# The first tile of an attention and mixing kernel put in written order: another order for the next batch, conversions dealt by a table, and three pairs of weight parts prepared ahead

## The chip, the cores and the metric

The kernel runs on one core of a Trainium2 chip. The metric is the device time of one execution in microseconds (us); the median of three runs before the change is 1008.54 us (1007.43 to 1009.77). The engines are TensorE (PE, with its weight loads PEld), VectorE (DVE), ScalarE (ACT) and GpSimd (POOL); SyncE (SP) issues most transfers. Each engine works through its own list of instructions in order; an instruction whose input is late holds all that are behind it on its engine.

## The reference, cut to what matters

Eight batches of 576 tokens and 512 columns (8 heads of 64). Two attentions in a row, a real part of a two-dimensional Fourier transform, a normalisation and a two-layer network:

```
p_packed = sm_attn(p, k, v)               # 32 packed rows per head
x = sm_attn(q, p_packed, p_packed)        # (B, S, 512) over all heads
u = x + real(fft(fft(x, axis=1), axis=2))
un = (u - mean(u)) / sqrt(var(u) + 1e-6)
out = u + relu(un @ w_ch1) @ w_ch2        # 512 -> 2048 -> 512
```

The two weights come as 64-bit floats: each element is fetched as two 32-bit words, and the kernel puts one fp32 number together from them.

## The kernel before, in words

**The network's tiles.** The 8 x 576 rows are 36 blocks of 128 rows, worked in 9 tiles of four blocks (`ffn`). A tile has 16 chunks of the hidden 2048 columns. For chunk j, `up(j)` multiplies the four turned blocks by a 512 x 128 piece of the first weight (12 matmuls of 128x512, into the one PSUM bank `ph`), ACT and DVE make the rectified result's two parts `hh` and `hl` from it, and `down(j)` multiplies these by a 128 x 512 piece of the second weight into the four banks `acc0` to `acc3` (again 12 matmuls). Every product is made of three, from a high and a low part of each operand. `down(j - 1)` stands behind `up(j)` in the program. At a tile's end the four banks are scaled, added to `u` and sent out, and the next tile's rows are turned (on PE as `untp`, or by transfers as `back`) and split into `uh` and `ul`.

**The weight parts.** `wsplits` is a generator: each `next(splits)` makes one pair `wr_h`, `wr_l` for the next piece, first weight and second weight in turn: a cast on ACT (L105) and a subtraction on POOL (L108). Six buffers hold them, so three pairs at most. Before the first `up` two pairs are made; after each `up` and each `down` one more. The pair that is made behind a product is thus used two products later.

**The mixing of the next batch.** While tile t runs, `front(t + 1)` makes the rows of batch t + 1: a generator that is taken one piece further at each of the 32 steps of a tile (`step(2 * j)` behind `up(j)`, `step(2 * j + 1)` behind `down(j - 1)`). Which piece comes at which step is written in the strings of `ORDER`: each letter is a part (s scores, t turned scores, p packed values, d their parts, g their spectrum, q queries, e and m the softmax's two halves, a its weights, f r h the folds), the digit the group of heads, and y a step's end. The first string is the prologue's (batch 0), the second that of batch 1, the third that of all later batches. The capitals S, X, U do both groups of heads in one part.

**The weights' conversion.** Batch 0's tile also has to put the weights together, for 16 chunks and two weights, which later tiles find ready in `w1f` and `w2f`. One conversion is a transfer of 512 KB into a staging place (`fetch`), two instructions on ACT (`top` L175 and `lows` L180) and one on DVE (`bits` L184). Staging places are parts of `w1f` and `w2f` that are not yet filled, two slots of `ubuf`, and two buffers `wst`. Two chunks are converted in the prologue; in the first tile `load_weights` converts one chunk (two parts) at every second step, up to chunk 15; the transfer of a part is issued with its conversion, or by the prologue's letter W for the first two chunks.

**What sets the order.** In the prologue and in the tiles 1 to 8 the order on PE, DVE, ACT and POOL is the program's (`tc.manual_schedule`). In tile 0 it is that of a scheduler that goes by its own costs, but for some ACT instructions that are kept in program order. The order on SP is the scheduler's everywhere. At the end of the conversions four DVE instructions (L193 to L200) compare one converted part against another way of making it.

Of the kernel before, what the change touches and what calls it, by code (L numbers as in the profile page):

```python
# [81 lines left out]
def tile_kernel(ctx, tc, kpT, qT, v, w1, w2, tabH, tabL, tabR, tabB, tabT, sel, ident_d, out):  # L82
# [103 lines left out]
    def load_weights(j):  # L186
        for n in range(2):
            tc.keep_in_program_order(top(j, n))
            proof = n == 1 and j == NJ - 1
            if proof:  # L190
                low = fetched[j, n][:, :, 0]
                want = work.tile([P, DM], I32, tag="tmp", name="want", bufs=3)
                nc.vector.tensor_scalar(want, low, 29, None, ALU.logical_shift_right)  # L193
            tc.keep_in_program_order(lows(j, n))
            if proof:
                off = small.tile([P, 1], F32, tag="nb", name="off")
                nc.vector.tensor_tensor(want, want, low, ALU.bitwise_xor)
                nc.vector.tensor_reduce(off, want, AX.X, ALU.max)
                st = stat_of[0, "E", 0]
                nc.vector.scalar_tensor_tensor(st[:, 2:3], off, 1e6, st[:, 2:3], ALU.mult, ALU.add)  # L200
# [836 lines left out]
```

## Time and profile before

| what | value |
|---|---|
| runs, median (lowest to highest) | 1008.54 us (1007.43 to 1009.77) |
| profiled execution, its own time | 1009.32 us |
| its span, first to last instruction | 1007.5 us |
| mean granted TensorE clock | 0.996 |
| moved from and to HBM | 55.58 MB read, 16.25 MB written |

The span runs from the first to the last instruction; the execution's own time is 1.8 us longer. A row of the view by stretches of time holds, from the left, the stretch, its length, the busy time of PE, PEld, DVE, ACT and POOL with the number of instructions, the granted clock, the share of the DMA engines and GB/s. A row of the timeline holds start, busy time of the group, engine, line, operation, destination and sources, and in brackets how long the engine sat idle before and whose event ended that. The busy time of a matmul is longer than its turn on PE, since they overlap: two 128x512 matmuls in a row start 0.23 us apart, though each has 0.39 us. So what a wait costs is read from the distance of two starts.

### The profile page before, as it was taken

The page shows a single profiled execution, that of the slowest core. Times are in us where ns is not written, and L with a number is a line of the kernel's source. Part 1 is how long each engine was busy: PE and PEld are TensorE (multiplying, and loading weights), DVE is VectorE, ACT ScalarE, POOL GpSimd, SP SyncE. Part 2 cuts the span into 40 slices and gives each one's busy share as a digit, 9 for nine tenths or more (in the row PEclk, how much of TensorE's full clock was granted, in tenths as well). Part 3 has the DMA queues.
Part 4 walks back from the last instruction along what each step waited for, and adds up shares of the span by engine and source line. Part 5 has one row for each costly group of instructions (what it writes and reads, how often), then busy time and mean ns, then how long its engine had stood idle before and what let it go on. Part 6 is the DMA issues. An engine that isn't in the chain of part 4 may idle for free.

```text
span 1007.5 us, 15129 instructions
## 1 busy us (share of the span) xinstructions
PE 972.9 (97%) x5706; PEld 792.4 (79%) x5706; DVE 592.7 (59%) x1187; ACT 441.4 (44%) x914; POOL 463.2 (46%) x413
## 2 busy tenths in 40 slices
PE   7899899999999999999999999999999999999998
PEld 4777577878877887788878888778778888887886
DVE  5865976578555946685657755694658452323112
ACT  4578465444444345343434443443433443233322
POOL 3236635454345534553545435543454354544443
PEclk9999999999999999999999999999999999999999
DMA  9337430410122003300231114110211010111001
GB/s 352 119 112 226 146 126 28 136 50 22 43 100 92 22 8 129 98 24 19 85 108 42 43 42 142 50 63 18 99 47 36 28 64 1 45 39 43 0 1 43
DMA packets 36938, 72.83 MB, mean 72 GB/s; under 512 B 4224, under 2 KB 18432, under 8 KB 36864
## 3 DMA queue, kind: packets, MB, share of 16 engines
q1 hardware_dynamic: 35856, 70.34, 20.6%
q0 software_dynamic: 1008, 1.51, 0.5%
q8 instruction: 45, 0.74, 0.3%
q14 instruction: 29, 0.24, 0.1%
HBM read 55.58 MB, written 16.25 MB: 71 GB/s over the span
## 4 chain that ended last, share of the span: by engine, by line
PE 74%; DVE 11%; issue 7%; POOL 4%; ACT 3%; DMA 1%; ACTq 0%; SPq 0%; POOLq 0%; DVEq 0%
PE ph L806 33%; PE acc L823 28%; POOL wr_l L108 3%; DVE turned L470 1%; PE po L367 1%; DVE turned L464 1%; PE s L306 1%; PE px L266 1%; PE px L264 1%; PE px L265 1%; DVE hl L813 1%; PE py L266 1%; PE e1tp L344 1%; PE pz L266 1%; PE pz L265 1%
## 5 line engine op out<-in xcount | busy, mean ns | idle before, releaser
L108 POOL TENSOR_TENSOR wr_l<-w1f,wr_h 128x512 fp32r<-128x512 f32 x144 | 188.7, 1313 | 395.4 <-ACT wr_h L105 391.5
L813 DVE SCALAR_TENSOR_TENSOR hl<-ph,hh 128x512 fp32r<-128x512 f32 x144 | 98.7, 685 | 303.6 <-ACT hh L812 303.3
L806 PE MATMUL ph<-uh,wr_h 128*128 128x512 f32 (+1 forms) x580 | 229.7, 396 | 9.8 <-DVE f L515 3.1
L108 POOL TENSOR_TENSOR wr_l<-w2f,wr_h 128x512 fp32r<-128x512 f32 x144 | 194.2, 1349 | 96.5 <-ACT wr_h L105 88.4
L823 PE MATMUL acc<-wr_l,hh 128*128 128x512 f32 x576 | 226.1, 393 | 6.5 <-POOL wr_l L108 6.4
L812 ACT ACTIVATE hh<-ph 128x512 fp32r<-128x512 f32 x144 | 86.1, 598 | 323.5 <-PE ph L806 323.5
L823 PE MATMUL acc<-wr_h,hh 128*128 128x512 f32 x576 | 226.3, 393 | 1.2 <-ACT wr_h L105 1.2
L806 PE MATMUL ph<-uh,wr_l 128*128 128x512 f32 (+1 forms) x580 | 226.6, 391 | 0.5 <-POOL wr_l L108 0.5
L806 PE MATMUL ph<-ul,wr_h 128*128 128x512 f32 (+1 forms) x580 | 226.3, 390 | 0.0
L823 PE MATMUL acc<-wr_h,hl 128*128 128x512 f32 x576 | 225.0, 391 | 0.0
L806 PEld LDWEIGHTS ph<-uh,wr_h 128*128 128x128 f32 x580 | 109.3, 188 | 46.3 <-issue 16.6
L823 PEld LDWEIGHTS acc<-wr_l,hh 128*128 128x128 f32 x576 | 108.2, 188 | 31.5 <-POOL wr_l L108 10.7
L806 PEld LDWEIGHTS ph<-uh,wr_l 128*128 128x128 f32 x580 | 109.3, 188 | 25.1 <-POOL wr_l L108 1.1
L823 PEld LDWEIGHTS acc<-wr_h,hh 128*128 128x128 f32 x576 | 108.1, 188 | 24.4 <-ACT wr_h L105 1.7
L823 PEld LDWEIGHTS acc<-wr_h,hl 128*128 128x128 f32 x576 | 108.1, 188 | 22.6
L806 PEld LDWEIGHTS ph<-ul,wr_h 128*128 128x128 f32 x580 | 109.3, 189 | 20.7
L105 ACT CAST wr_h<-w2f 128x512 fp32r<-128x512 f32 x144 | 89.3, 620 | 0.0
L105 ACT CAST wr_h<-w1f 128x512 fp32r<-128x512 f32 x144 | 88.4, 614 | 0.8 <-DVE w1f L184 0.6
L240 ACT ACTIVATE junk<-ubuf,stat 128x512 f32<-128x512 f32 x36 | 25.8, 719 | 53.3 <-DVE stat L235 53.3
L108 POOL TENSOR_TENSOR gl<-turned,gh 128x516 fp32r<-128x516 f32 x14 | 21.7, 1553 | 16.3 <-ACT gh L105 16.3
L682 DVE SCALAR_TENSOR_TENSOR ubuf<-qe,pe 128x512 f32<-128x512 f32 x32 | 27.1, 883 | 0.5
L470 DVE TENSOR_TENSOR turned<-turned 128x258 f32<-128x258 f32 x32 | 26.9, 881 | 0.4
(213 smaller groups left out, 1282.9 us busy)
## 6 DMA issues: line engine op xcount, KB each, us to landing
kp<-kpT SPq DMA_DIRECT2D x16, 608.0 KB, 4.9
out<-ubuf SPq DMA_DIRECT2D x36, 256.0 KB, 2.1
vt<-v SPq DMA_DIRECT2D x14, 640.0 KB, 4.8
wst<-w SPq DMA_DIRECT2D x17, 512.0 KB, 4.3
qt<-qT SPq DMA_DIRECT2D x14, 576.0 KB, 4.6
far<-unt SPq DMA_DIRECT2D x26, 256.0 KB, 2.0
back<-far SPq DMA_DIRECT2D x104, 64.0 KB, 2.0
ubuf<-w SPq DMA_DIRECT2D x9, 512.0 KB, 4.3
```

Source lines behind the costliest of these rows:

```text
L105: copied = nc.scalar.copy(hi, src)
L108: (lo_eng or nc.vector).tensor_tensor(lo, src, hi.bitcast(F32), ALU.subtract)
L240: nc.scalar.activation(junk, u, AF.Square, bias=st[:, 1:2], scale=-sign, accum_out=st[:, 2:3])
L264: nc.tensor.matmul(o, lh, rh, start=first, stop=False)
L265: nc.tensor.matmul(o, lh, rl, start=False, stop=False)
L266: nc.tensor.matmul(o, ll, rh, start=False, stop=last)
L470: TW[TA[min(b, 2)]].tensor_tensor(prod[0][:, t, :], prod[0][:, t, :], prod[1][:, t, :], ops[t])
L682: nc.vector.scalar_tensor_tensor(u_of[key], qe, sign, pe, ALU.mult, ALU.add, accum_out=stat_of[key][:, 0:1])
L806: nc.tensor.matmul(ph[:, t], l[:, c * P:(c + 1) * P], r[:, c, t], start=(k == 0), stop=(k == 11))
L812: nc.scalar.activation(hh[:, :T], ph[:, :T], AF.Relu)
L813: nc.vector.scalar_tensor_tensor(hl[:, :T], ph[:, :T], 0.0, hh[:, :T].bitcast(F32), ALU.max, ALU.subtract)
L823: nc.tensor.matmul(acc[i], l[:, w], r, start=(j == 0 and k == 0), stop=(j == NJ - 1 and k == 2))
```

## The change

Six things are changed.

1. **Order of tile 0.** Tile 0 is put in `tc.manual_schedule` like the others: PE, DVE, ACT and POOL follow the program.
2. **The next batch's pieces.** The second string of `ORDER` is dropped, and batch 1 uses the third one, that of the later batches, with S, X and U for both groups together.
3. **Conversions by a table.** `TAKES` says for each of tile 0's 32 steps how many of the 27 conversions that are left behind the prologue are made there: 16 of them at the steps 2 to 11, one each at 12, 13, 14, 16, 18 and 21 to 24.
4. **Staging by a table.** `STAGES` gives each of the 32 parts its staging place; nine are fetched by the prologue (letters W0 to W8 in place of W0 to W3), and `fetch_free`, called with each conversion, fetches ahead as soon as the place of the next part is free.
5. **Three pairs.** Before the first `up` three pairs of weight parts are made and not two, so that a pair made behind a product is used three products later, in every tile.
6. **Small ones.** In the prologue two `lows` and three `bits` stand earlier and the conversion of the part (2, 0) is added; the first `up` does its 12 matmuls in another order; the comparison (L193 to L200) is gone.

```diff
 ORDER = ("... v0 z0 T2 W4 W5 W6 W7 W8 q0 e0 p1 "
-         "... i64 j1 F1 u1 u2 u3 h1 J1 X0 "
-         "H1 P1",
-         "s0 s1 y y t0 y t1 y p0 y y y d0 p1 y q0 d1 y y g0 y g1 y e0 q1 e1 y m0 y m1 y a0 a1 y f0 r0 h0 y "
-         "y f1 r1 h1",
+         "... i64 j1 u1 u2 F1 u3 h1 J1 v1 v2 X0 "
+         "H1 v3 P1",
          "S y X y p0 p1 y d0 d1 y g0 y U y g1 y e0 y e1 y y m0 y a0 y m1 y a1 y f0 y r0 y h0 y f1 y r1 y "
          "h1 y y")
-STG0 = [-2, -2, -4, -4, -6, -6]
-STG1 = [9, None, None]
+STAGES = [-2, -2, -4, -4, -6, -6, 9, 0, 1, -2, -2, -4, -4, -6, -6, 9, 0, 1, ...]
+TAKES = [1, 1, 2, 1, 2, 2, 2, 1, 2, 1, 1, 2, 1, 1, 1, 0, 1, 0, 1, 0, 0, 1, 1, 1, 1, 0, ...]
...
+    def fetch_free():
+        while line:
+            j, n = line[0]
+            i = STAGES[2 * j + n]
+            if last_in.get((i, i < 0 and n)) in fetched:
+                break
+            fetch(j, n)
...
-    def load_weights(j):
-        for n in range(2):
-            tc.keep_in_program_order(top(j, n))
...
+    def load_weights(count):
+        for j, n in todo[:count]:
+            top(j, n)
+            lows(j, n)
             bits(j, n)
+            fetch_free()
+        del todo[:count]
...
-        for x in ORDER[min(b, 2)].split():
+        for x in ORDER[min(b, 1)].split():
...
-                    c, (l, r) = k // 3, ((wh, uh), (wh, ul), (wl, uh))[k % 3]
+                    if step < T:
+                        c, (l, r) = k % 4, ((wh, uh), (wl, uh), (wh, ul))[k // 4]
+                    else:
+                        c, (l, r) = k // 3, ((wh, uh), (wh, ul), (wl, uh))[k % 3]
...
             if at == "means":
+                top(LEAD, 0)
+                lows(LEAD, 0)
                 turn_blocks(0, 1)
...
-        bits(1, 0)
         turn_blocks(2, 3)
         cur.parts(2)
         cur.parts(3)
+        bits(*todo.pop(0))
         next(splits)
-        bits(0, 1)
-        bits(1, 1)
+        next(splits)
...
-            if t == 0 and i % 2 == 0 and i // 2 + LEAD < NJ:
-                load_weights(i // 2 + LEAD)
+            if t == 0:
+                load_weights(TAKES[i])
...
-        with tc.manual_schedule(engines=MANUAL) if t > 0 else nullcontext():
+        with tc.manual_schedule(engines=MANUAL):
             ffn(first, cur, step, nxt, t + 1 >= B)
```

Three places show the order that results. The first is PE where the prologue passes into tile 0: `untp` turns the four blocks, `pz` is the rest of batch 0's mixing (step 0), `ph` is the first `up`. Before:

```order
L763 MATMUL untp<-ident,un 128x128 x4
L264 MATMUL pz<-yh,tbh_94 128x258
L265 MATMUL pz<-yl,tbh_94 128x258
L763 MATMUL untp<-ident,un 128x128 x4
L266 MATMUL pz<-yh,tbl_96 128x258
L264 MATMUL pz<-yh,tbh_94 128x258
```

and with the change:

```order
L763 MATMUL untp<-ident,un 128x128 x8
L809 MATMUL ph<-uh,wr_h 128x256 x4
L809 MATMUL ph<-uh,wr_l 128x256 x4
L763 MATMUL untp<-ident,un 128x128 x8
L809 MATMUL ph<-ul,wr_h 128x256 x4
L809 MATMUL ph<-uh,wr_h 128x256 x4
L809 MATMUL ph<-uh,wr_l 128x256 x4
L809 MATMUL ph<-ul,wr_h 128x256 x4
L264 MATMUL pz<-yh,tbh_94 128x258
```

The 14 `pz` matmuls stood between the turned blocks and now stand behind the whole first `up`, whose products without `ul` come first.

The second place is DVE in the middle of tile 0, where batch 1's softmax is finished for the first group of heads (`s_1099`; its `d` and `z` products are on POOL), ahead of the folds. With the change:

```order
L194 SCALAR_TENSOR_TENSOR w1f<-w1f,ubuf 128x512
L816 SCALAR_TENSOR_TENSOR hl<-ph,hh 128x512
L243 TENSOR_SCALAR stat<-stat 128x1
L441 TENSOR_REDUCE z_1264<-s_1099 128x18
L442 TENSOR_SCALAR d_1265<-z_1264 128x18
L443 TENSOR_SCALAR z_1264<-z_1264 128x18
L444 RECIPROCAL z_1264<-z_1264 128x18
L194 SCALAR_TENSOR_TENSOR w2f<-w2f,wst 128x512
L484 STREAM_TRANSPOSE a<-s_1099 128x576
L194 SCALAR_TENSOR_TENSOR w1f<-w1f,wst 128x512
L816 SCALAR_TENSOR_TENSOR hl<-ph,hh 128x512
```

Before, the last group's transpose and the first group's folds stood together with two conversions in front of one `hl`:

```order
L482 TENSOR_TENSOR s_1265<-s_1265,z_1328 128x576
L184 SCALAR_TENSOR_TENSOR w1f<-w1f,wst 128x512
L184 SCALAR_TENSOR_TENSOR w2f<-w2f,ubuf 128x512
L484 STREAM_TRANSPOSE a<-s_1265 128x576
L528 MEMSET f 128x3x2
L547 SCALAR_TENSOR_TENSOR xl<-eo,xh 128x256
L549 TENSOR_TENSOR ol<-eo,oh 128x256
L515 TENSOR_TENSOR f<-eo 128x2x3x15
L519 TENSOR_TENSOR f<-a 128x3 x2
L515 TENSOR_TENSOR f<-eo 128x2x3x15
L526 COPY f<-eo 128x2x3
L813 SCALAR_TENSOR_TENSOR hl<-ph,hh 128x512
```

The conversions have moved ahead of the folds, and the transpose `a` stands between two `hl` behind a chain on POOL.

The third place is ACT at the end of a later tile (tile 1), from the last `hh` on; `back` and `untp` are the next tile's rows. Before:

```order
L812 ACTIVATE hh<-ph 128x512
L105 CAST uh<-back 128x4x128 x2
L105 CAST wr_h<-w2f 128x512
L105 CAST wr_h<-w1f 128x512
L105 CAST uh<-back 128x4x128
L105 CAST uh<-untp 128x4x128
L105 CAST wr_h<-w1f 128x512
```

and with the change:

```order
L815 ACTIVATE hh<-ph 128x512
L103 CAST uh<-back 128x4x128 x2
L103 CAST wr_h<-w1f 128x512 x2
L103 CAST uh<-back 128x4x128
L103 CAST uh<-untp 128x4x128
L103 CAST wr_h<-w2f 128x512
```

The cast of the last piece of the second weight, `wr_h<-w2f`, stood behind two casts of `uh` and is no longer there: it is made one product earlier, ahead of `hh`.

More of the change, by code (lines that the diff above doesn't have):

```diff
@@ L1 @@
-from contextlib import ExitStack, nullcontext
+from contextlib import ExitStack
 import numpy as np
@@ L38 @@
 TL = (0, 0, 0)
-ORDER = ("K0 K1 V0 I0 Q0 V1 W0 Q1 B0 W1 W2 W3 i70 s0 x0 s1 i40 t0 x1 p0 b0 T0 t1 n0 w0 u0 d0 T1 i20 v0 z0 T2 q0 e0 p1 "
-         "b1 i80 l0 d1 w1 w2 w3 m0 q1 a0 e1 g0 i122 f0 r0 F0 l1 m1 n1 g1 i203 a1 j0 h0 J0 H0 P0 f1 r1 i64 j1 F1 u1 u2 u3 h1 J1 X0 "
-         "H1 P1",
-         "s0 s1 y y t0 y t1 y p0 y y y d0 p1 y q0 d1 y y g0 y g1 y e0 q1 e1 y m0 y m1 y a0 a1 y f0 r0 h0 y "
-         "y f1 r1 h1",
+ORDER = ("K0 K1 V0 I0 Q0 V1 W0 Q1 B0 W1 W2 W3 i70 s0 x0 s1 i40 t0 x1 p0 b0 T0 t1 n0 w0 u0 d0 T1 i20 v0 z0 T2 W4 W5 W6 W7 W8 q0 e0 p1 "
+         "b1 i80 l0 d1 w1 w2 w3 m0 q1 a0 e1 g0 i122 f0 r0 F0 l1 m1 n1 g1 i203 a1 j0 h0 J0 H0 P0 f1 r1 i64 j1 u1 u2 F1 u3 h1 J1 v1 v2 X0 "
+         "H1 v3 P1",
          "S y X y p0 p1 y d0 d1 y g0 y U y g1 y e0 y e1 y y m0 y a0 y m1 y a1 y f0 y r0 y h0 y f1 y r1 y "
          "h1 y y")
-STG0 = [-2, -2, -4, -4, -6, -6]
-STG1 = [9, None, None]
+STAGES = [-2, -2, -4, -4, -6, -6, 9, 0, 1, -2, -2, -4, -4, -6, -6, 9, 0, 1, -2, -2, -4, -4, 9, 0, 1, -2, -2, 9, 0, 1, 9, 0]
+TAKES = [1, 1, 2, 1, 2, 2, 2, 1, 2, 1, 1, 2, 1, 1, 1, 0, 1, 0, 1, 0, 0, 1, 1, 1, 1, 0, 0, 0, 0, 0, 0, 0]
 LEAD = 2
@@ L124, in tile_kernel @@
     idles = [psf.tile([P, 512], F32, tag="ph", name="idle")]
-    stages = (STG0 + STG1 * 40)[:2 * NJ]
     tbh = [cpool.tile([P, KT], F32R, name=f"tbh{t}") for t in range(2)]
@@ L153, in spot @@
         return t[:, 0:size].rearrange("p (a n) -> p a n", a=shape[1])
+    line = [(j, n) for j in range(NJ) for n in range(2)]
+    last_in = {}
     def fetch(j, n):
-        i = stages.pop(0)
-        if i is None:
+        assert line.pop(0) == (j, n)
+        i = STAGES[2 * j + n]
+        assert last_in.get((i, i < 0 and n)) not in fetched
+        last_in[i, i < 0 and n] = j, n
+        if i < 0:
+            st = spot(n, i, [P, 512, 2]).bitcast(I32)
+        elif i < 2:
             st = work.tile([P, 512, 2], I32, tag="wst", name="wst", bufs=2)
-        elif i < 0:
-            st = spot(n, i, [P, 512, 2]).bitcast(I32)
         else:
@@ L164, in fetch @@
         fetched[j, n] = st
+    def fetch_free():
+        while line:
+            j, n = line[0]
+            i = STAGES[2 * j + n]
+            if last_in.get((i, i < 0 and n)) in fetched:
+                break
+            fetch(j, n)
     def chunk(j, n):
@@ L169, in top @@
     def top(j, n):
-        if (j, n) not in fetched:
-            fetch(j, n)
         high, c = fetched[j, n][:, :, 1], chunk(j, n)
@@ L184, in bits @@
         nc.vector.scalar_tensor_tensor(c, c, 3, low, ALU.logical_shift_left, ALU.bitwise_or)
-    def load_weights(j):
-        for n in range(2):
-            tc.keep_in_program_order(top(j, n))
[L189 to L200, printed above, removed]
+    todo = [(j, n) for j in range(LEAD, NJ) for n in range(2)]
+    def load_weights(count):
+        for j, n in todo[:count]:
+            top(j, n)
+            lows(j, n)
             bits(j, n)
+            fetch_free()
+        del todo[:count]
     u_of, stat_of, place_of, free = {}, {}, {}, list(range(NU))
```

## The prediction

> **What bounds the kernel now.** I read the first page, the stretches by tile, PE's waits, and then the timelines around the waits. Page and stretches (one row for tile 0 from its first whole `up`, one each for tiles 1 and 2):
>
> ```profile
> span 1007.5 us, 15129 instructions
> PE 972.9 (97%) x5706; PEld 792.4 (79%) x5706; DVE 592.7 (59%) x1187; ACT 441.4 (44%) x914; POOL 463.2 (46%) x413
> 53.00:176.26 123.26, 114.02 (x658) 88.70 (x656) 87.23 (x170) 80.62 (x165) 61.93 (x54) 0.99 0.41 130
> 176.26:283.81 107.55, 106.81 (x650) 87.81 (x648) 72.28 (x147) 47.18 (x100) 49.51 (x42) 1.00 0.18 59
> 283.81:391.36 107.55, 106.80 (x649) 87.76 (x648) 70.87 (x143) 46.48 (x98) 50.30 (x43) 1.00 0.17 60
> ```
>
> PE sets the end: it is busy 97% and its tiles follow each other without a break. So only what shortens PE's own list or its waits counts. Tile 0 takes 123.3 us where tile 1 takes 107.55 with the same kind of work: nearly 16 us more. The other engines are busier in tile 0 (DVE 87 against 72, ACT 81 against 47) but not full over the whole of it. PE's waits in tile 0, and then from tile 1 to the end (total, times, longest):
>
> ```profile
> PE ph L806 <- ACT wr_h L105: 2.9, 1, 2.9
> PE acc L823 <- POOL wr_l L108: 1.7, 3, 0.9
> PE ph L806 <- DVE hl L813: 1.5, 1, 1.5
> PE py L264 <- ACT fh L538: 1.5, 1, 1.5
> PE acc L823 <- ACT wr_h L105: 1.2, 1, 1.2
> ...
> PE acc L823 <- POOL wr_l L108: 4.8, 7, 0.8
> PE ph L806 <- DVE f L515: 3.1, 2, 1.6
> ```
>
> Tile 0 has 8.8 us of them, most between 107 and 133 us, where DVE's list carries the folds and conversions at once. Later, one kind comes back seven times: the last `down` of tiles 1 to 7 waits for POOL's `wr_l`.
>
> **Tile 0, by the length of tile 1.** With the change tile 0 has the calls of tile 1 in the order of tile 1, so the PE list of tile 1 is the measure of it, from the first `pz` behind the first `up` to the next tile's first `ph`:
>
> ```profile
> 176.26 0.40 PE L806 MATMUL ph<-uh,wr_h 128*128 128x512 f32 x1
> 178.99 0.28 PE L264 MATMUL pz<-yh,tbh 128*128 128x258 f32 x1
> 283.81 0.39 PE L806 MATMUL ph<-uh,wr_h 128*128 128x512 f32 x1
> ...
> 279.32 0.48 PE L823 MATMUL acc<-wr_h,hh 128*128 128x512 f32 x1
> 279.67 0.48 PE L823 MATMUL acc<-wr_l,hh 128*128 128x512 f32 x1
> ```
>
> From 178.99 to 283.81 are 104.8 us. Tile 0 turns all four of its successor's blocks on PE, tile 1 only one: 12 transposes more. Between the last two rows stands one transpose, and they are 0.35 us apart where 0.23 is usual: 0.12 each, 1.4 us together. Tile 1 holds 0.6 us of a wait at its end that goes (below). So tile 0 without new waits lasts 104.8 + 1.4 - 0.6 = 105.6 us from its first `pz`.
>
> That `pz` now stands behind the first `up`. Two rows say when this can end:
>
> ```profile
> 48.26 1.33 ACT L888 ACTIVATE un<-ubuf,stat 128x512 f32<-128x512 f32 x2 [1.61 <-DVE stat L235]
> 53.44 0.59 ACT L105 CAST uh<-untp 128x512 fp32r<-128x512 f32 x1 [0.23 <-PE untp L763]
> 57.76 0.73 PE L823 MATMUL acc<-wr_h,hh 128*128 128x512 f32 x2 [1.19 <-ACT wr_h L105]
> ```
>
> The added `top` and `lows` of part (2, 0) need 1.1 us of ACT (start to start 0.56 each, below) and stand where ACT idled 1.61 us: nothing, with DVE's statistics as the cover; without it 1.1 us, on the path. The earlier `lows` and `bits` fall into the time in which ACT and DVE wait for the fold's high part; nothing too. The last `uh` is ready at 53.44 + 0.59 = 54.0; the second half of `up`, 12 half-wide matmuls at 0.12, ends at 55.5. The 1.19 us before 57.76 go, since the third pair's cast now stands ahead of `hh`. So tile 1 would begin at 55.5 + 105.6 = 161.1 and not at 176.26: **15.1 us less**, without new waits. This holds the shorter scores of both groups together and the lost half clock behind the longest wait:
>
> ```profile
> 116.10 0.55 PE L806 MATMUL ph<-uh,wr_h 128*128 128x512 f32 x1 [2.88 <-ACT wr_h L105]
> 119.82 0.40 PE L806 MATMUL ph<-uh,wr_h 128*128 128x512 f32 x1
> ```
>
> Nine starts in 3.72 us where 0.23 each is usual: 1.7 us lost after PE had idled 2.88.
>
> **The tile ends.** Here is one of the seven, on PE, ACT and POOL:
>
> ```profile
> 495.08 0.39 PE L823 MATMUL acc<-wr_h,hh 128*128 128x512 f32 x1
> 496.28 0.50 PE L823 MATMUL acc<-wr_l,hh 128*128 128x512 f32 x1 [0.81 <-POOL wr_l L108]
> 492.56 0.60 ACT L812 ACTIVATE hh<-ph 128x512 fp32r<-128x512 f32 x1 [1.18 <-PE ph L806]
> 493.05 1.13 ACT L105 CAST uh<-back 128x512 fp32r<-128x512 f32 x2
> 494.08 0.62 ACT L105 CAST wr_h<-w2f 128x512 fp32r<-128x512 f32 x1
> 494.78 1.44 POOL L108 TENSOR_TENSOR wr_l<-w2f,wr_h 128x512 fp32r<-128x512 f32 x1 [3.93 <-ACT wr_h L105]
> ```
>
> The cast stands behind `hh` and two `uh`, so POOL ends at 496.2 and PE's second matmul starts 1.20 us after its first, 0.97 late. With three pairs this cast and its `wr_l` are made a whole product (12 matmuls, 2.74 us) earlier: 2.74 of room against 0.97 of lateness. The 4.8 us of waits cost some 0.16 more each by that same pair of starts (0.97 against 0.81): 4.8 + 7 x 0.16 = **5.9 us less**. What is late next is nothing by these rows; the new pair's buffer comes free only at the product's end, so its cast now waits for PE, with the next step's ACT work behind it: 47 us of ACT in 107 leave room for that.
>
> **What written order may cost in tile 0.** Sixteen conversions stand in the steps 2 to 11, five chunks. Their prices, and the rows of the POOL chain:
>
> ```profile
> 113.27 0.66 ACT L175 ACTIVATE w1f<-wst 128x512 f32<-128x512 f32 x1
> 114.38 0.66 ACT L175 ACTIVATE w2f<-ubuf 128x512 f32<-128x512 f32 x1
> L184 DVE SCALAR_TENSOR_TENSOR w1f<-w1f 128x512 int32<-128x512 int32 x2 | 1.4, 682 | 0.0
> L184 DVE SCALAR_TENSOR_TENSOR w1f<-w1f,wst 128x512 int32<-128x512 int32 x8 | 7.1, 887 | 5.6 <-ACT wst L180 5.5
> L184 DVE SCALAR_TENSOR_TENSOR w2f<-w2f 128x512 int32<-128x512 int32 x3 | 3.1, 1053 | 0.0
> L445 POOL TENSOR_TENSOR s<-s,d 128x576 f32<-128x576 f32 x1 | 1.3, 1337 | 0.0
> L108 POOL TENSOR_TENSOR wr_l<-w1f,wr_h 128x512 fp32r<-128x512 f32 x17 | 22.6, 1330 | 34.0 <-ACT wr_h L105 30.9 <-DVE d L442 3.1
> L482 POOL TENSOR_TENSOR s<-s,z 128x576 f32<-128x576 f32 x1 | 1.2, 1162 | 0.8 <-DVE s L422 0.8
> L484 DVE STREAM_TRANSPOSE a<-s 128x576 f32<-128x576 f32 x2 | 1.5, 772 | 0.0
> ...
> wst<-w SPq DMA_DIRECT2D x17, 512.0 KB, 4.3
> ```
>
> Five chunks last 5 x 107.55 / 16 = 33.6 us. ACT does tile 1's work in them, 47.18 x 5 / 16 = 14.7, and 16 x 1.11 of conversions (113.27 to 114.38): 32.5 of 33.6. DVE: 72.28 x 5 / 16 = 22.6 and 16 x 0.68 to 0.89: 33.5 to 36.8. So DVE runs level or up to 3.2 us over; I take the middle, 1.6. Behind it comes the chain of the first group: DVE's `z` and `d` (about 1.0), then on POOL `s<-s,d` 1.34, a `wr_l` 1.33, `s<-s,z` 1.16, then on DVE `a` 0.77, a conversion 0.68 and only then `hl` 0.69, all in one line because DVE waits in front of `a`: 7.0 us between two `hl`. PE needs the next one after an `up` and a `down`, 2 x 2.74 = 5.5: 1.5 us late. For the folds behind it I add 1.4, the size of one of today's waits there. New waits: 1.6 + 1.5 + 1.4 = **4.5 us**, spread, so no lost clock. Bounds: nothing, if the slack of `ph` takes them; 12 us, if each of 27 conversions takes 1.05 on DVE and not 0.68 (10.0) and the chain's 1.5 comes on top, rounded up. I take a value at the lower part, since the waits today came with two conversions and the folds in one chunk, which is what is pulled apart. Transfers: nine parts stand ready from the prologue, each takes 4.3 us to land, and its place is free several steps before its turn: nothing. The dropped comparison stands in DVE idle time: nothing.
>
> [...]
>
> **The sum.** 15.1 + 5.9 - 4.5 = 16.5 us less. Of the profiled execution's 1009.32 that leaves 992.8; it stood 0.8 above the median, so 992 to 993: I say **993 us**.
>
> **The rivals.**
> 1. *The two waits of 1.6 us spread.* They stand in tiles 5 and 6 where `hl` comes late behind DVE instructions that take longer while a `wr_l` runs, as here the second against the first:
>
> ```profile
> 666.34 0.48 DVE L733 TENSOR_SCALAR unp<-ubuf,stat 128x512 f32<-128x512 f32 x1
> 672.51 1.57 DVE L733 TENSOR_SCALAR unp<-ubuf,stat 128x512 f32<-128x512 f32 x1
> ```
>
> Three pairs move every `wr_l`; if one such wait falls in each of tiles 1 to 7, 5 x 1.7 = 8.5 us come back: 1001.5. For it: the same list gave a wait in two tiles and none in five, so the phase decides. Against: the number of `wr_l` is the same.
> 2. *Tile 0 is bound by DVE.* New waits of 12 us, the bound above: 1000.5. For it: DVE is level with PE in five chunks. Against: over the whole tile it is not full.
> 3. *The third pair isn't really held*, because its cast waits for a buffer and is then as late as before: the tile ends keep their 5.9 us: 999. Against: it has a whole product more.
> 4. *Slower.* One mechanism: in tile 0's written order ACT's and DVE's conversions stand in front of `hh` and `hl`, and what they take shows on PE instead of beside it. A conversion is 1.11 + 0.68 = 1.8 us; it decides from the point where more than 21.0 / 27 = 0.78 us of each is seen. At half, 24 us: 1012. For it: both engines' lists are nearly full there. Against: the two work on different conversions at once, and `ph` leaves them one `down` of room each chunk.
>
> **How the numbers follow.** The forecast has 0.56, by itself 988 (no new waits) to 998; the rivals in their order 0.14, 0.14, 0.06 and 0.10. A measurement of this kernel tells about 0.2% from no change, 2 us. The forecast and rivals 1 to 3 are faster, together 0.90, less 0.04 for a tail of rival 2 that ends near the old time; slower is rival 4. Range: 987 to 1003 leaves out rival 4 and the edges of the others.
>
> **What would show it.** Tile 1's first `ph` near 166 us and not 176 (161 without new waits); no wait of `acc` on POOL's `wr_l` at the tile ends, tiles of some 106.8 us and not 107.55; in tile 0 short waits of `ph` on `hl` around chunks 6 to 8; no slow clock there. Tiles 1 to 7 of over 108 us would show rival 1; a wait of `acc` that stays, rival 3; tile 0 longer than 123 us, rival 4, and the forecast wrong.

## The result, and the profile of the changed kernel

| | kernel before | changed kernel |
|---|---|---|
| runs, median (lowest to highest) | 1008.98 us (1007.43 to 1009.98) | **999.36 us** (996.71 to 1002.41) |
| ratio, 95% interval | | **0.9908** (0.9884 to 0.9932) |
| profiled execution: its own time, span | 1009.32, 1007.5 us | 1002.41, 1000.6 us |
| tile 1's first `ph` starts at | 176.26 us | 178.95 us |
| from there to the end of the span | 831.2 us | 821.7 us |

The kernel before was run five times in all here; the three runs of the first table are among them. The time fell by 9.6 us, and 993 us were forecast, with 987 to 1003 as the range. The last two rows say more than the first: the whole gain stands behind tile 0. Tile 0 and the prologue, from which 10.6 us were expected, take 2.7 us longer in the profiled execution, which is the slowest of the five.

From the changed kernel's page, and two of its stretches (tile 0 from its first `pz` to tile 1's first `ph`, then tile 1 to tile 2's first `ph`; the columns are as before):

```profile
PE 970.3 (97%) x5706; PEld 797.6 (80%) x5706; DVE 565.3 (56%) x1183; ACT 450.9 (45%) x914; POOL 472.3 (47%) x413
58.75:178.95 120.20, 109.84 (x651) 88.74 (x649) 78.07 (x161) 78.88 (x159) 62.55 (x54) 0.97 0.35 115
178.95:285.32 106.37, 106.37 (x650) 87.78 (x648) 67.88 (x146) 47.84 (x100) 52.00 (x44) 1.00 0.18 61
```

Tile 1 has no idle PE left (106.37 busy of 106.37) and is 1.2 us shorter than the 107.55 of the kernel before. Tile 0 has 10.4 us of idle PE and a mean clock of 0.97. PE's waits, first three kinds from the list of the whole changed kernel, then (last two rows) all that is left from tile 1 on:

```profile
PE ph L809 <- DVE hl L816: 7.6, 5, 2.2
PE ph L809 <- DVE stat L243: 3.2, 1, 3.2
PE s2Tt L306 <- DMA qt<-qT: 1.9, 1, 1.9
...
PE ph L809 <- DVE hl L816: 3.0, 2, 1.5
PE ph L809 <- DVE ul L106: 0.5, 1, 0.5
```

The seven waits of `acc` on `wr_l` are gone. So is a kind that the prediction did not count, six waits of `ph` on the transposed scores, in the kernel before from tile 1 on:

```profile
PE ph L806 <- DVE s L422: 2.3, 6, 0.4
```

The reason is in the groups by line for the same stretch, the kernel before first (two rows), then the changed one:

```profile
L470 DVE TENSOR_TENSOR turned<-turned 128x258 f32<-128x258 f32 x24 | 21.7, 944 | 0.4
L429 DVE TENSOR_TENSOR s<-s,m 128x576 f32<-128x576 f32 x12 | 11.1, 924 | 0.4
L429 DVE TENSOR_TENSOR s<-s,m 128x576 f32<-128x576 f32 x12 | 15.9, 1328 | 0.4
L470 DVE TENSOR_TENSOR turned<-turned 128x258 f32<-128x258 f32 x24 | 9.2, 424 | 0.4
```

The join `turned` (L470) stands on DVE right ahead of the transposes that free the bank for which `ph` waits. It took 944 ns on the mean where a `wr_l` ran on POOL beside the first of each two (414 ns at the shortest, 1483 at the longest), and takes 424 now, with no `wr_l` beside it. The `wr_l`, made one product earlier, runs beside L429 instead, which takes longer there (924 to 1328 on the mean) and which nothing on PE waits for. So the same overlap of DVE and POOL is there as before, and here its move worked for the change. With 6 x 0.16 us for these waits (an estimate by the tile end in the prediction, where a wait of 0.81 us made the next start 0.97 late), their 2.3 us and the 5.9 us of the tile ends make 9.2 of the 9.6 us.

**What tile 0 lost.** The largest wait there ends at 108.92. On ACT, DVE and PE, with the stretch by which ACT is judged:

```profile
95.00:110.00 15.00, 11.83 (x53) 9.48 (x52) 9.88 (x16) 13.54 (x27) 9.57 (x8) 1.00 0.39 115
100.31 0.69 ACT L432 ACTIVATE s<-s 128x576 f32<-128x576 f32 x1 [1.40 <-POOL s L429]
105.25 0.64 ACT L185 ACTIVATE w2f<-w2f 128x512 f32<-128x512 f32 x1
106.89 0.65 ACT L190 ACTIVATE ubuf<-ubuf 128x512 int32<-128x512 uint8 x1
107.44 0.57 ACT L815 ACTIVATE hh<-ph 128x512 fp32r<-128x512 f32 x1
108.18 0.68 DVE L816 SCALAR_TENSOR_TENSOR hl<-ph,hh 128x512 fp32r<-128x512 f32 x1
108.92 0.50 PE L809 MATMUL ph<-uh,wr_h 128*128 128x512 f32 x1 [3.17 <-DVE stat L243]
```

The row names `stat`, a small instruction behind `hl`; what is late is `hl`, because `hh` stands on ACT behind two conversions (the row at 105.25 begins them, that at 106.89 ends them). ACT comes to them late: it is busy 13.5 of these 15 us, and of the 1.46 us in which it is not, 1.40 stand in one piece ahead of 100.31, where it waits for a subtraction of the scores on POOL. So two things make this wait, ACT's conversions and the scores' way over POOL; the experiments below take them apart. The next wait, 2.25 us at 116.90, is the chain that the prediction had written down:

```profile
109.62 0.37 DVE L442 TENSOR_SCALAR d<-z 128x18 f32<-128x18 f32 x1
110.43 1.63 POOL L445 TENSOR_TENSOR s<-s,d 128x576 f32<-128x576 f32 x1
112.02 1.30 POOL L106 TENSOR_TENSOR wr_l<-w1f,wr_h 128x512 fp32r<-128x512 f32 x1
113.28 1.15 POOL L482 TENSOR_TENSOR s<-s,z 128x576 f32<-128x576 f32 x1
114.47 0.78 DVE L484 STREAM_TRANSPOSE a<-s 128x576 f32<-128x576 f32 x1 [3.43 <-POOL s L482]
116.17 0.68 DVE L816 SCALAR_TENSOR_TENSOR hl<-ph,hh 128x512 fp32r<-128x512 f32 x1
```

From `hl` to `hl` are 116.17 - 108.18 = 8.0 us, where 7.0 were forecast. The other new stops of PE in tile 0 are 2.1 us at 83 (by the row of waits the second transfer of queries; e4 below corrects that), 1.6 us at 129 and 1.0 us at 136 (folds in front of `hl`), by the starts of its matmuls. With 3.3 and 2.4 us for the two above that makes 10.4 us, not 4.5. On top of it come stretches at half clock: over 5 us the granted clock is 0.76 and 0.78 from 40 and from 50 us, 0.70 from 85 and 0.77 from 115, where the kernel before has one such stretch (0.66 from 115).

### The profile page after: what moved, and what is told of

It reads as the page before. It is cut to its first block, busy times and chain, and to the rows that moved or that the text cites. A ratio compares the mean times of both kernels' runs of the same rounds, so it can differ in the third digit from the quotient of the medians.

```text
span 1000.6 us, 15241 instructions
## 1 busy us (share of the span) xinstructions
PE 970.3 (97%) x5706; PEld 797.6 (80%) x5706; DVE 565.3 (56%) x1183; ACT 450.9 (45%) x914; POOL 472.3 (47%) x413
## 3 DMA queue, kind: packets, MB, share of 16 engines
q1 hardware_dynamic: 35856, 70.34, 20.5%
## 4 chain that ended last, share of the span: by engine, by line
PE 86%; DVE 9%; ACT 2%; DMA 1%; issue 1%; POOL 1%; SPq 0%; ACTq 0%; POOLq 0%; DVEq 0%
PE ph L809 37%; PE acc L826 35%; DMA w1f<-w 1%; PE po L367 1%; DVE hl L816 1%; PE px L266 1%; PE px L264 1%; DVE s L482 1%; PE px L265 1%; PE py L266 1%; PE py L265 1%; PE py L264 1%; PE pz L264 1%; PE pz L265 1%; PE pz L266 1%
## 5 line engine op out<-in xcount | busy, mean ns | idle before, releaser
L106 POOL TENSOR_TENSOR wr_l<-w2f,wr_h 128x512 fp32r<-128x512 f32 x144 | 188.5, 1309 | 307.8 <-ACT wr_h L103 303.8
L106 POOL TENSOR_TENSOR wr_l<-w1f,wr_h 128x512 fp32r<-128x512 f32 x144 | 200.7, 1394 | 185.3 <-ACT wr_h L103 170.0
L872 DVE SCALAR_TENSOR_TENSOR ubuf<-acc,stat,ubuf 128x512 f32<-128x512 f32 x36 | 24.5, 742 | 2.2 <-PE acc L826 2.2
L106 DVE TENSOR_TENSOR yl<-py,yh 128x258 fp32r<-128x258 f32 x32 | 13.3, 426 | 19.1 <-ACT yh L103 18.2
L244 POOL TENSOR_TENSOR stat<-stat,mhalf 128x1 f32<-128x1 f32 x36 | 22.9, 649 | 0.8 <-DVE stat L243 0.8
```

Source lines behind the costliest of these rows:

```text
L106: (lo_eng or nc.vector).tensor_tensor(lo, src, hi.bitcast(F32), ALU.subtract)
L244: nc.gpsimd.tensor_tensor(st[:, 2:3], st[:, 2:3], mhalf, ALU.pow)
L872: nc.vector.scalar_tensor_tensor(u, acc[i], stat_of[key][:, 2:3], u, ALU.mult, ALU.add)
```

## The experiments

Theory A, formed on this comparison: the later tiles' 9.6 us are the pairs' alone; tile 0's order was worth about 15 us on PE's list and gave them back through waits (a chain over POOL, ACT's list of conversions) and the half clock behind some of them (6.8 us from 30 us on, 1.7 in the kernel before). The rivals are in the expectations. All twelve runs:

| run | median, us | ratio to the kernel before (95%) | tile 1's first `ph` |
|---|---|---|---|
| changed kernel | 999.36 | 0.9908 (0.9884 to 0.9932) | 178.95 |
| e1_pairs_only | 999.14 | 0.9901 (0.9886 to 0.9916) | 175.33 |
| e2_two_pairs | 1009.42 | 1.0006 (0.9991 to 1.0021) | 176.38 |
| e3_chain_on_dve | 996.81 | 0.9876 (0.9858 to 0.9895) | 175.14 |
| e4_queries_first | 1000.20 | 0.9911 (0.9884 to 0.9937) | 178.03 |
| e5_one_each | 997.76 | 0.9886 (0.9870 to 0.9903) | 173.45 |
| e6_later_tiles_engines | 995.09 | 0.9856 (0.9839 to 0.9872) | 170.55 |
| e7_prologue_back | 997.98 | 0.9888 (0.9872 to 0.9905) | 176.9 |
| e8_prologue_pz | 995.39 | 0.9859 (0.9845 to 0.9874) | 170.8 |
| e9_folds_kept_free | 991.30 | 0.9818 (0.9803 to 0.9833) | 167.43 |
| e10_more_early | 992.49 | 0.9830 (0.9817 to 0.9844) | 169.4 |
| e11_free_at_transposes | **988.98** | **0.9797** (0.9784 to 0.9811) | 164.48 |
| e12_old_pieces | 1005.98 | 0.9964 (0.9950 to 0.9978) | 182.54 |

### The pairs without the order, and the order without the pairs

e1, an edit of the kernel before:

```
             if t == 0 and i % 2 == 0 and i // 2 + LEAD < NJ:
                 load_weights(i // 2 + LEAD)
+            if t == 0 and i == 29:
+                next(splits)
```

> The kernel before, with one edit: in chunk 14 of tile 0 one more pair of weight parts is made ready, so that tiles 1 to 7 hold three pairs; tile 0's order and the prologue stay. Theory A (the later tiles' gain is the pairs' alone, tile 0 gained nothing): no wait of acc on wr_l at the tile ends, from tile 1's first ph to the end 821.7 us instead of 831.2, tile 1's first ph still near 176, the whole at 0.990 to 0.991 of the kernel before, level with the changed kernel. Theory B (the pairs give only the waits seen of acc, 4.8 us, or the predicted 5.9, and the rest of the later tiles' 9.6 comes with the written order): 825 to 826 us and 0.994 to 0.995. If a third pair is not really held: 831 us and 1.000.

e2, an edit of the changed kernel, at the end of the prologue:

```
         next(splits)
-        next(splits)
```

> The changed kernel with two pairs held instead of three, everything else as changed. Theory A: the waits of acc on wr_l come back at the tile ends, from tile 1's first ph to the end near 831 us instead of 821.7, and the time is 9 to 10 us above the changed kernel, some 1009 us, level with the kernel before; tile 1's first ph stays near 179. Theory B (written order in tile 0 is worth something by itself, hidden in the profiled execution by its clock): 1003 to 1006 us. A further 1 to 2 us would be lost in tile 0 if the third pair also covers waits there.

PE's waits from tile 1 on in e1 (whole list without one of 0.5 us), then in e2:

```profile
PE ph L806 <- DVE hl L813: 3.0, 2, 1.5
...
PE acc L826 <- POOL wr_l L106: 4.8, 7, 0.8
PE ph L809 <- DVE hl L816: 3.1, 2, 1.6
PE ph L809 <- DVE s L422: 2.3, 6, 0.4
```

In e1, 997.0 - 175.33 = 821.7 us lie behind tile 1's first `ph`, in e2 1007.6 - 176.38 = 831.2: the two numbers of the table above, each to a tenth. The one `next(splits)` makes the whole difference of 9.5 us, with the waits on the scores included, and the whole written order of tile 0 is worth nothing on the mean (e2 1.0006; the changed kernel, 0.9908, is no better than e1, 0.9901). Theory A holds; theory B of both falls. One number of theory A for e2 is missed: tile 1's first `ph` stands at 176.38 and not near 179. That execution lost 3.4 us to half clock from 30 us on, the changed kernel's 6.8.

"On the mean" is needed. Executions of e2 at a mean granted clock of 0.996 and 0.998 took 1007.0 and 1006.4 us, those at 0.989 to 0.990 took 1012.2 to 1012.7; the kernel before took 1008.6 to 1009.7 at 0.997. One execution each at 0.997 took 996.7 us of the changed kernel and 999.2 of e1. So by these few executions the order gains some 2.5 us where the clock holds, and loses them where more half clock comes (6.8 us from 30 us on in the profiled execution of the changed kernel, at 0.990).

### The parts of tile 0's loss, one at a time

e3:

```
-EN = ((0, 1), (1, 0), (0, 0))
-EW = ((0, 0), (1, 0), (0, 0))
+EN = ((0, 1), (0, 0), (0, 0))
+EW = ((0, 0), (0, 0), (0, 0))
```

> The changed kernel with the subtraction of the maximum, the subtraction of the mean and the scaling of the first group's scores in tile 0 on DVE instead of POOL (later tiles already do that). Theory C (the way from DVE to POOL and back, behind a wr_l each time, is what makes hl late at 114 and, through the exponentials, at 105): the 2.4 us at 114 go, of the 3.3 us at 105 half or more goes, tile 1's first ph 3 to 5 us earlier (174 to 176), time 994 to 997 us. Theory D (DVE is level with PE in these chunks, so three instructions of some 0.8 us more on it make hl late elsewhere): tile 1's first ph within 1 us of 179, time 998 to 1001 us.

e4, in the second string of `ORDER`:

```
-         "S y X y p0 p1 y d0 d1 y g0 y U y ...
+         "S y X y p0 p1 Q0 Q1 y d0 d1 y g0 y U y ...
```

> The changed kernel with both transfers of tile 0's queries issued directly one after the other on SP, ahead of two transfers of weights that wait for a conversion on DVE; nothing else moves. Theory E (the 2.1 us at 83 are the second transfer's, which stands 3.2 us behind the first): the wait of s2Tt on qt goes, tile 1's first ph 1.5 to 2 us earlier, time 997 to 998 us, unless it is lost in the noise of 1 to 2 us. Theory F (PE then waits as long for hl, since ACT and DVE are behind by then): the wait changes its name, tile 1's first ph stays within 0.7 us of 179.

PE after the two waits in e3, and the wait at 83 to 87 in e4:

```profile
107.77 0.50 PE L809 MATMUL ph<-uh,wr_h 128*128 128x512 f32 x1 [1.35 <-DVE stat L243]
114.65 0.50 PE L809 MATMUL ph<-uh,wr_h 128*128 128x512 f32 x1 [1.11 <-DVE hl L816]
...
86.40 0.79 PE L809 MATMUL ph<-uh,wr_h 128*128 128x512 f32 x1 [2.17 <-DVE s L422]
```

e3 took the waits from 3.17 and 2.25 to 1.35 and 1.11 us. Its prologue ends as that of e4 (last `px` at 47.66 and 47.72), so tile 1's first `ph` is compared between these two: 2.9 us earlier. Theory C holds in its time, at the slow edge of its range (996.81), and in the first wait, of which more than half goes without any conversion being moved. What is left of that one stands behind ACT's conversions, which end at 106.4 with `hh` next. The second wait, which theory C let go altogether, is only halved: with the chain on DVE, DVE works without a pause from one `hl` (107.03) to the next (113.92), and two conversions of 1.79 and 0.98 us are in it. In e4 the transfer's wait is gone and a wait on the scores' transposes has its place, because two conversions and the join stand ahead of these on DVE; the time did not move (1000.20 against 999.36). Theory F holds in its cause: the transfer was not what ended that stop. It named `hl` where the scores' transposes came, and its number is narrowly missed: tile 1's first `ph` is 0.9 us earlier and not within 0.7, but the prologue of that execution ends 1.6 us earlier (last `px` at 47.72 against 49.35).

e5:

```
-TAKES = [1, 1, 2, 1, 2, 2, 2, 1, 2, 1, 1, 2, 1, 1, 1, 0, 1, 0, 1, 0, 0, 1, 1, 1, 1, 0, 0, ...]
+TAKES = [1] * 27 + [0] * 5
```

> The changed kernel with its conversions in tile 0 dealt one to each of the first 27 steps (the changed kernel deals up to two to a step and is up to six ahead of that). Theory G (ACT, which works without a pause from 95 to 109 us, has two conversions in front of hh at 105, and DVE two in front of the score transposes at 85): the waits of 3.3 us at 105 and of some 3.9 us at 83 to 87 shrink by half or more, tile 1's first ph 3 us earlier or more, time 995 to 997 us. Theory H (a conversion in written order costs the same wherever it stands, and now some stand among the folds): these waits shrink, those of 1.6 and 1.0 us at 129 and 136 grow by one conversion of 0.7 us each and new ones come behind them; time 998 to 1001 us.

PE's stretch from the first `pz` to tile 1's first `ph`, in e4 and then in e5:

```profile
57.13:178.03 120.90, 112.02 (x650) 89.88 (x649) 78.22 (x161) 79.07 (x159) 61.63 (x54) 0.96 0.35 114
56.03:173.45 117.42, 108.33 (x650) 87.58 (x649) 79.10 (x161) 79.29 (x159) 61.08 (x54) 0.99 0.36 118
```

Both theories saw something. The 3.17 us shrank to 1.5 and the stop at 83 to 87 by about half, while the two waits at the folds grew from 1.44 and 0.83 to 2.10 and 1.40, by the 0.7 us of a conversion each. In sum PE idles 9.1 us of its stretch, against 10.4 in the changed kernel and 8.9 in e4, which saved no time. Tile 1's first `ph` stands 4.6 us before that of e4, but that is no more than the half clock: from 30 us on it cost 1.7 us in this execution and 6.9 in that of e4. The time (997.76) lies between the theories, and its interval overlaps that of the changed kernel. So one conversion to each step mainly moved the waits; whether it also makes half clock rarer is not shown.

e7, in the first string of `ORDER`:

```
-... i64 j1 u1 u2 F1 u3 h1 J1 v1 v2 X0 H1 v3 P1
+... i64 j1 F1 u1 u2 u3 h1 J1 X0 H1 v1 v2 v3 P1
```

> The changed kernel with the prologue's two low parts and three bit steps back behind the fold's high part and behind the last subtraction, as before the change stood. Theory I (two bit steps on DVE slow POOL's and DVE's fold instructions beside them, fh is 0.45 us late, and PE's wait of 1.2 us is now and then followed by half clock): the wait of py on fh is 0.6 us as before, no half clock from 42 to 46 us, the last px of the prologue starts 0.5 us earlier than in executions without the half clock there (47.7) and 2 us earlier than in those with it (49.35); time 0.5 to 1.5 us less, 998 to 999 us. Theory J (the bit steps then stand in front of the splits of uh, or make the second pair late): the first ph comes 0.7 us or more later, nothing gained.

First the reason for this run: PE in the prologue of the changed kernel, the last instruction of the fold on POOL there, and the same in the kernel before.

```profile
41.46 0.39 PE L264 MATMUL py<-gh,fh 128*128 128x258 f32 x1 [1.20 <-ACT fh L538]
42.75 0.42 PE L264 MATMUL py<-gh,fh 128*101 128x258 f32 x1
39.98 0.56 POOL L530 TENSOR_SCALAR f<-a 128x31 f32<-128x31 f32 x1
39.85 0.23 POOL L530 TENSOR_SCALAR f<-a 128x31 f32<-128x31 f32 x1
```

The moved `bits` run on DVE from 39.15 to 40.44, POOL's last two instructions of the fold take twice as long beside them (0.49 and 0.56 us for 0.23 each), `fh` comes 0.45 us later, and PE's waits of 1.20 and 0.50 us are followed by matmuls at half clock (0.21 us from start to start, 0.12 in e7; the granted clock is 0.76 over these 5 us). In e7 PE waits 0.62 us for `fh`, and no half clock stands from 40 to 60 us. But the last `px` starts at 47.59, hardly earlier than in e3 and e4, which have the longer wait without half clock (47.66, 47.72): the `bits` now stand ahead of a split, for which PE waits 0.31 us. So the edit saves no time of its own; what it may take away is the half clock, some 1.6 us in those executions that have it (49.35 in the changed kernel). Its median is 1.4 us below the changed kernel's, within the scatter of both. Theory I is half right: the cause is, the 0.5 us are not.

### Together

e6: the edits of e4 and e5, and all of batch 1's scores and folds on DVE (as e3, and `EF`):

```
-EF = (((0, 0, 0, 0), (0, 0, 0, 0)), ((1, 1, 1, 1), (0, 0, 0, 0)), ...
+EF = (((0, 0, 0, 0), (0, 0, 0, 0)), ((0, 0, 0, 0), (0, 0, 0, 0)), ...
```

> The changed kernel with three edits: all of the first group's scores work and folds in tile 0 on DVE, as in the later tiles (the three instructions of e3_chain_on_dve and the four folds), conversions one to each step, queries' transfers side by side. Theory C with G: the 2.9 us that e3_chain_on_dve moved tile 1's first ph against e4_queries_first, 1.6 us at 129 (hl behind a 2.6 us fold on DVE that shares its time with POOL), some 3 us at 105 and 2 to 4 us at 83 to 87: tile 1's first ph 8 to 10 us before 178, time 989 to 992 us. Theory D (DVE is then level with PE and hl late in each chunk from 5 to 11): tile 1's first ph near 174, time 995 to 998 us.

e8: e6 and e7 together, and in the prologue:

```
         turn_blocks(2, 3)
+        next(gen0)
         cur.parts(2)
```

> All edits of e6_later_tiles_engines and of e7_prologue_back, and the rest of batch 0's mixing (the two pz) put back into the time in which PE waits for the last two turned blocks, ahead of the first up's second half. Theory K (PE idle in the first up, 0.7 and 0.2 us beside the 1.4 us in front of it, brings half clock at 50 to 55, which costs 1.7 us each time): no half clock between 40 and 60 us, first up and pz done 1.5 to 3 us earlier than in e6_later_tiles_engines, time 2 to 3 us less than that. Theory L (ACT has to copy the two pz in front of the last two uh, so the first up's second half comes as much later): within 0.7 us of e6_later_tiles_engines.

e6 came to 995.09 us, where theory D had put it, with the waits on `hl` that D had named; its first `ph` of tile 1 (170.55) lies between the two. The wait at 105 us, 3.17 in the changed kernel, 1.35 with the scores on DVE (e3) and 1.48 with the conversions dealt one by one (e5), is 0.41 with both (the queries' edit alone left 2.83, e4): each of the two takes away a cause of its own. Its stretches show the new bound, DVE (third busy time) at 14.7 and 14.8 of 15 us; the two rows behind are those of e9, below:

```profile
100.00:115.00 15.00, 12.35 (x52) 9.25 (x52) 14.73 (x25) 10.16 (x19) 7.97 (x7) 1.00 0.47 140
115.00:130.00 15.00, 13.13 (x56) 10.44 (x55) 14.79 (x35) 10.23 (x20) 7.04 (x5) 0.97 0.35 104
...
100.00:115.00 15.00, 14.59 (x65) 11.66 (x64) 12.43 (x22) 9.20 (x17) 8.07 (x7) 1.00 0.23 70
115.00:130.00 15.00, 14.56 (x65) 11.67 (x64) 13.68 (x37) 9.87 (x20) 6.76 (x5) 1.00 0.28 81
```

e8 is level with e6 (995.39), as theory L said: the wait that the `pz` were to fill, 0.20 us ahead of the second half of the first `up` in e6, grew to 0.97 because ACT copies the `pz` ahead of the last two `uh`, and another came at 68. On PE in e8:

```profile
56.74 0.74 PE L809 MATMUL ph<-uh,wr_h 128*128 128x256 f32 x4 [0.97 <-ACT uh L103]
68.41 0.50 PE L809 MATMUL ph<-uh,wr_h 128*128 128x512 f32 x1 [1.06 <-DVE hl L816]
```

e9 (e6 and e7, with another table) and e10 (a third table):

```
e9:  TAKES = [1, 1, 2, 1, 2, 2, 1, 1, 1, 1, 1, 1, 0, 0, 1, 0, 1, 0, 1, 1, 1, 1, 1, 1, 1, 1, 1, 1, 0, ...]
e10: TAKES = [1, 2, 2, 2, 2, 2, 1, 1, 1, 1, 1, 1, 0, 0, 1, 0, 0, 1, 0, 1, 1, 1, 1, 1, 1, 1, 1, 0, ...]
```

> The edits of e6_later_tiles_engines and e7_prologue_back, with the conversions of tile 0 dealt so that none or one in two steps stands among the scores and folds (15 by step 11, then 3 in the steps 12 to 18, then one each to step 27). Theory M (DVE is what is late from 100 to 130 us in e6_later_tiles_engines, where it is busy 14.7 and 14.8 of each 15 us, and each bit step of 0.7 to 1.8 us taken from there comes off the waits on hl of 1.3, 1.2 and 2.0 us and the half clock behind the last, 1.7 us): four to five bit steps fewer, tile 1's first ph 3 to 6 us earlier than 170.6, time 989 to 992 us. Theory N (the conversions only move their price: ACT is late at 95 to 100, where 12.8 of 15 us are full, or the later bit steps make wr_h late): 994 to 996 us.

> As e9_folds_kept_free, but with 11 and not 9 conversions in the first six steps and 17 by step 11. Theory M: one or two bit steps fewer among the folds and behind them, level with e9_folds_kept_free or up to 1 us faster. Theory O (the parts are then not yet there: each takes 4 to 7 us from issue to landing and its place comes free only with an earlier conversion, so ACT waits for a transfer with hh behind it): waits of ph on hl between 58 and 83 us, where there are none in any run so far, 1 to 3 us slower than e9_folds_kept_free.

e9: 991.30 us, tile 1's first `ph` at 167.43, DVE at 12.4 and 13.7 of 15, waits on `hl` in tile 0 of 0.4 us each. Theory M holds: it was DVE's list, and what was taken from it came off PE's waits (from the first `pz` to tile 1 PE idles 3.0 us, in e6 6.4). In e10 tile 1's first `ph` is 2.0 us later than in e9 and the median 1.2 us higher, though the two intervals overlap. There is a new wait between 58 and 83, as theory O said, but not the one that it named and not for its reason: PE waits 1.41 us at 67 (0.28 in e9) for `xa`, which stands on DVE right behind `hl`. ACT in e9 and in e10 at the place:

```profile
63.70 0.66 ACT L190 ACTIVATE ubuf<-ubuf 128x512 int32<-128x512 uint8 x1
64.26 0.59 ACT L815 ACTIVATE hh<-ph 128x512 fp32r<-128x512 f32 x1
...
63.97 0.68 ACT L185 ACTIVATE w2f<-wst 128x512 f32<-128x512 f32 x1
65.09 0.61 ACT L815 ACTIVATE hh<-ph 128x512 fp32r<-128x512 f32 x1
```

No transfer is waited for; the second conversion of step 1 stands on ACT in front of `hh`, which is 0.83 us later, and with it `hl` and `xa`, although the prologue ended 0.26 us earlier.

e11, a fourth table (the same 15 conversions by step 11):

```
e11: TAKES = [1, 1, 2, 2, 2, 1, 0, 1, 2, 1, 1, 1, 0, 0, 1, 0, 1, 0, 1, 1, 1, 1, 1, 1, 1, 1, 1, 1, 0, ...]
```

> As e9_folds_kept_free, with the same 15 conversions by step 11 dealt so that one and not two stand in step 5 and none in step 6, just ahead of the transposes of the scores for which the next ph waits. Theory R (one conversion on DVE, 0.7 us, ahead of these transposes is what makes PE wait 1.6 us at 83 in e9_folds_kept_free, and that wait brings the half clock from 84.5 to 88, 1.7 us): wait of ph on s under 0.9 us, no half clock from 84 to 88, tile 1's first ph 2.5 to 3.5 us before 167.4, time 988 to 989 us. Theory S (the scores' bank and the transposes themselves, 1.3 us behind two instructions of 1.3 and 0.8 us, set it): the wait stays over 1.2 us, half clock or not, time 990.5 to 992 us.

PE in e9 (the wait and the half clock behind it, 0.63 us for a matmul that takes 0.39 in e11), then in e11, with its stretch from the first `pz` to tile 1's first `ph`:

```profile
84.47 0.76 PE L809 MATMUL ph<-uh,wr_h 128*128 128x512 f32 x1 [1.58 <-DVE s L422]
85.03 0.63 PE L809 MATMUL ph<-ul,wr_h 128*128 128x512 f32 x1
...
82.97 0.50 PE L809 MATMUL ph<-uh,wr_h 128*128 128x512 f32 x1 [0.85 <-DVE s L422]
55.54:164.48 108.94, 106.43 (x650) 86.48 (x649) 80.95 (x168) 78.33 (x159) 55.23 (x47) 1.00 0.39 127
```

988.98 us, 20.5 us below the kernel before, run beside it (1009.43, ratio 0.9797), and 10.4 below the changed kernel's median; theory R holds in each of its numbers. Two conversions, moved by two steps each away from the transposes, come with 2.9 us at tile 1's start: about 1.7 are the half clock behind the wait in e9, 0.7 the wait itself, and 0.3 were there already when the prologue ended.

### The order of the pieces

e12, the changed kernel with its table of conversions and three pairs, and the kernel before's list of pieces for batch 1 as a second of three strings:

```
-        for x in ORDER[min(b, 1)].split():
+        for x in ORDER[min(b, 2)].split():
```

> The changed kernel with the next batch's pieces in tile 0 in the list that the kernel before names for it (each group's scores, queries and folds in steps of their own), written order, conversions and three pairs as changed. Theory T (the later tiles' list, with both groups' scores and queries in one step each, is worth the few us that shorter narrow products give, and costs the wait on s at 83 to 87 with its half clock): that wait is gone, PE's busy time in tile 0 longer by 2 to 5 us, tile 1's first ph within 2 us of 178, time 997 to 1002 us. Theory U (the order of pieces decides tile 0): tile 1's first ph more than 4 us later or earlier.

1005.98 us: tile 1's first `ph` is 4.5 us later than 178, as theory U has it. Theory T had the wait at 83 to 87 right (it is gone), and missed this:

```profile
136.16 0.58 PE L266 MATMUL py<-gh,fh 128*128 128x258 f32 x1 [6.15 <-ACT fh L540]
```

That list does the second group's folds and the products that need them in one step, so in written order `py` comes on PE before DVE has done the folds (it begins them at 131.3). The kernel before, with the same list in the scheduler's order, waits 1.5 us at most for `fh` there. A wait of 2.71 us at 62, for the softmax's `e`, is new too. So a list made for the scheduler costs 3.6 us in written order by the two profiled executions, 5.6 by the ratios and 6.6 by the medians, and the later tiles' list is what makes written order level with the scheduler here at all.

## Why the prediction was right, and where it was not

The time is inside the range and 6 us above the number. That is partly luck, since two errors of opposite sign make it: the smaller term, the tile ends, gave 9.6 us for 5.9, and the larger one, tile 0's 10.6 us, gave nothing (2.7 us lost in the profiled execution, 1.0006 on the mean in e2).

- **The tile ends** (5.9 us less). The mechanism is confirmed: e1 and e2 move nothing but the third pair, and the waits go and come back. The size is 9.5 us, and tile 1 lasts 106.4 us where 106.8 were forecast. The term that was too small is "5.9 us less": the six waits on the scores went too, because a `wr_l` no longer runs beside the join.
- **Tile 0 without new waits** (15.1 us less, tile 1's first `ph` at 161.1). The template holds to 1 us: in e11 the first `pz` behind the first `up` starts at 55.54, where 55.5 was worked out, and from there to tile 1 are 108.9 us, of which 2.5 are waits, where 105.6 were forecast without waits. In the changed kernel that `pz` starts at 58.75. The step that failed is "The earlier `lows` and `bits` fall into the time in which ACT and DVE wait for the fold's high part; nothing too": beside the `bits` the fold itself is slower on POOL (0.56 us for 0.23 in its last instruction), and half clock came behind the waits that follow, in the prologue and the first `up` (granted clock 0.76 from 40 us and 0.78 from 50 us, over 5 us each). That is 3.2 us in the profiled execution, and 0.3 to 0.5 in e6 and e5, which have the same prologue without that half clock (`pz` at 55.80 and 56.03).
- **New waits in tile 0** (4.5 us, bounds 0 and 12). Measured: 10.4 us. The chain over POOL was named and came out at 2.4 us for 1.5, the folds at 2.6 for 1.4. The term "1.6" for DVE was given to the wrong engine: DVE was busy 9.9 of 15 us at that place, ACT 13.5, and 3.3 us came there, from ACT's conversions in front of `hh` and from ACT's own wait for POOL. The sum for ACT, 32.5 of 33.6 us, stood in the prediction and was taken as room; it is a mean over five chunks, and within them the conversions came in twos. The 2.1 us at 83 are in no term: there DVE has two conversions and the join ahead of the transposes for which PE waits.
- **"Spread, so no lost clock"** is wrong: 6.8 us are lost to half clock behind 30 us in the profiled execution, against 1.7 in the kernel before; 3.4 of them fall before the first `pz`, 3.4 behind the waits that end at 87 and 117.
- **The sum for tile 0.** Tile 1's first `ph` was forecast at 161.1 + 4.5 = 165.6 and stands at 178.95. The 13.3 us between are 3.2 of a late first `pz`, 5.9 of waits beyond the 4.5, 3.4 of half clock in tile 0, and 0.8 by which the template is short, in e11 as here.
- **A sign that did appear.** "Tile 0 longer than 123 us" was to show rival 4 and the forecast wrong. From its first `up` at 52.93 to tile 1 it lasts 126.0 us in the profiled execution. For tile 0 the forecast was wrong there; the whole came out faster because of the tile ends.
- **Transfers** (nothing): right by e4, which gave the queries their place and gained nothing.
- **The rivals.** 1: both waits of 1.5 us stand in the same two tiles as before, none is added. 2: its price (12 us of new waits, 1000.5) is the nearest to what was measured, but its reason did not hold: DVE became the bound only in e6, when ACT's and POOL's causes were gone. 3: the third pair is held. 4: its mechanism, conversions in front of `hh` seen on PE, is a part of what happened at 105 us, at a smaller price than its 24 us.

## What to carry to other kernels

When work is dealt into another engine's written list, look at each place for what stands right behind it there and who waits for that: the sum over five chunks left room on ACT, and 10 us of waits came all the same. Dealing alone did not cure it, since the scores' way over POOL was a second cause (e5); with that gone, three tables for the same 27 conversions gave 995.1, 991.3 and 989.0 us (e6, e9, e11; the last two also have the edit of e7, which saved no time of its own). Count a wait on the matmul engine at its length plus the half clock that may follow it, 1.7 us each time here. The join on DVE took 944 ns on the mean where a subtraction ran on POOL beside the first of each two, and 424 where none did, so moving the one also decides which instruction pays for it, and that should be one for which nobody waits.
